# Two of a step's sums of g blocks, moved from VectorE to accumulating DMA transfers

## The chip, the cores and the metric

The kernel runs on one core of a Trainium2 chip. The metric is the device time of one execution in microseconds; the time before is the median of three runs. A profile of one execution shows when each instruction of each engine ran: TensorE (PE, with its weight loads as PEld), VectorE (DVE), ScalarE (ACT), GpSimd (POOL), and SyncE (SP), which only issues transfers.

## The reference

A convolution along the sequence with seven softmax-normalised taps per head, then a feed-forward block without gate or bias; all in float32.

```python
w = softmax(weight, axis=-1)                 # 8 heads x 7 taps
out = einsum('hk,bskhg->bshg', w, x_unf)     # x: 8 x 4096 x 192, causal, 24 columns a head
x2 = out.reshape(32768, 192)
h = x2 @ w_in                                # 192 x 2048
g = h * (1 / (1 + exp(-1.702 * h)))          # quick GELU
return g @ w_out                             # 2048 x 192
```

## The kernel before

The tokens are worked in 32 steps ("big" in the code). A step holds 512 tokens from each half of the batch. Step 0 has a routine of its own (`first_step`, with the loading and rounding of the weights); steps 1 to 31 each run `hidden` twice, with v = 0 and v = 1, and then `second`.

- `hidden(big, v, ...)` makes half of the hidden columns. The products with w_in (line 577, through `product1`) follow a scheme that needs fewer products than blocks and, in exchange, sums of blocks before and after. ScalarE copies (line 607) and VectorE sums (line 611, through `sum2`) put the results together in `room`, and ScalarE's quick GELU writes them to `g` (lines 598 and 600).
- `second(big, ...)` multiplies g with w_out by a scheme on blocks: g is seen as rows 1 to 3 of five 128-row pieces and columns 1 to 4 of 256 tokens, and `block(r, j)` is such a block, 128 partitions x 5 x 256 numbers, 640 KB. Sixteen sums or differences of blocks go before the products p2 to p20. Each product is one call of `go(bank, h, w, t, ...)` (matmuls on line 867): five rounds, or six with `left`, and in each round three matmuls for the product and one of a list of side products, in four column strips of the array.

Every engine's order of work is the order in which the code calls it (`tc.manual_schedule()`); the waits between engines and transfers follow from which tiles are read and written. `work(us)` and `vec_work(us)` put pieces of the next step's convolution between VectorE's sums, as many as fit a stated time.

Around the change, the order is this. Late in `hidden` with v = 1, line 679 makes t_a = block(2,3) - block(3,3), and line 690 sums k18; then line 692 adds block(2,2) into block(2,3), and line 693 makes t_8. Then `give(False, big)` lets line 516 (`cross`) issue copies of the next step's convolved blocks from one half of the partitions to the other, on SyncE's queue; these wait for the last products that read `conv_t`. In `second`, TensorE runs p3, p11, p2 (on t_a), p19 (on block(2,3)), p8, p10, and the product called q13p (on t_a). VectorE meanwhile does lines 893, 896, 897 and 900; line 903, which adds block(2,2) into t_a after p2 has read it; line 908, which reads p8; and line 910, t_8 = t_a - block(3,2). Block (2,2) is rewritten on line 913. GpSimd in these steps adds the convolution's taps (line 505) and sums convolved blocks (lines 388 and 390).

Transfers that add into their destination exist in the kernel before in one place: `add_forms` (line 439), twelve of 240 KB each, issued by GpSimd in step 0.

Of the kernel before, what the change touches and what calls it, by code (L numbers as in the profile page):

```python
# [11 lines left out]
ALU = mybir.AluOpType  # L12
# [3 lines left out]
def kernel(  # L16
# [29 lines left out]
    nc = tc.nc  # L46
# [34 lines left out]
    vec, act = nc.vector, nc.scalar  # L81
# [42 lines left out]
    def block(r, j):  # L124

        n, o = COL[j]
        i = ND * ROW[r]
        return g[:, n, i : i + ND, o * T : (o + 1) * T]

    def rest(j):  # L130
# [16 lines left out]
    t_a, t_8 = (  # L147
        flat_room[:, i * BLK : (i + 1) * BLK].rearrange("p (k t) -> p k t", k=ND) for i in range(2)
    )
# [76 lines left out]
    def form(i):  # L226
        return w_form[:, i, :, :]
# [82 lines left out]
    for c in range(NC):  # L310
        part = sel[:, c, :].rearrange("i (h q) -> i h q", h=2)
        for sign in (1, -1):
            nc.gpsimd.affine_select(
                out=part,
                in_=part,
# [220 lines left out]
    def give(early, big):  # L536
        given[early] = big
        for what in waiting[early]:
            cross(*what)
        waiting[early].clear()  # L540
# [45 lines left out]
    def terms(big, v, slot, *ts, first=False):  # L586
        for t in ts:
            product1(slot, *TERMS[t], big, v, first)
            first = False
# [3 lines left out]
    def gelu(b, u, v, src):  # L593
        m, n = divmod(b, 2)
        i = 2 * (v * len(PAIRS) + PAIRS.index((m, u)))
        if isinstance(src, list):
            for h in range(2):
                act.activation(g[:, n, i + h, :], src[h], AF.Gelu_apprx_sigmoid)  # L598
        else:
            act.activation(g[:, n, i : i + 2, :], src, AF.Gelu_apprx_sigmoid)  # L600
# [4 lines left out]
    def copy2(dst, src):  # L605
        for h in range(2):
            act.copy(bank(dst, h), bank(src, h))  # L607

    def sum2(op, dst, a, b):
        for h in range(2):  # L610
            op(*(bank(t, h) for t in (dst, a, b)))  # L611
# [6 lines left out]
    def hidden(big, v, x, z, y, sums, work, fetch, last=lambda: None):  # L618

        def pe(slot, *ts, first=False):
            terms(big, v, slot, *ts, first=first)


        if v:
            pe(z, 7, first=True)
            give(True, big)
        pe(sums, 12)
        copy2(k15, sums)  # L630
        pe(x, 5, 17)
        gelu(B11, 0, v, x)
        if not v:
            pe(z, 7, first=True)
        pe(sums, 0)
        copy2(k16, sums)
        last()
        def turn_next():
            if big + 2 < N_BIG:
                need(f"done {big + 1}")  # L640
                turn_x(big + 2)

        if v or big == 1:
            work(3.2 if v else 1.6)

        pe(y, 6, 14, first=True)
        sum2(vec.tensor_sub, x, z, k15)
        if v:
            vec.tensor_add(t_s, block(2, 1), block(2, 4))
            vec.tensor_sub(block(2, 1), block(2, 1), block(3, 1))  # L650
        work(2.6 if v else 1.2)
        pe(sums, 13)
        copy2(k19, sums)
        pe(x, 2)
        copy2(k18, x)
        pe(z, 11)
        pe(sums, 20, 10)
        sum2(vec.tensor_sub, k15, y, k19)
        gelu(B12, 0, v, sums)
        pe(x, 4)  # L660
        copy2(k20, x)
        sum2(vec.tensor_sub, k19, z, k19)
        work(1.1)
        gelu(B22, 1, v, k19)
        gelu(B22, 0, v, k15)
        pe(y, 8)
        pe(sums, 1, 9, first=True)
        pe(y, 15)
        if v and big == 1:
            turn_next()  # L670
        else:
            work(2.2 if big > 1 and not v else 1.1)
        sum2(vec.tensor_add, k20, k20, sums)
        sum2(vec.tensor_sub, k16, y, k16)
        gelu(B11, 1, v, k20)
        pe(x, 18)
        gelu(B21, 1, v, x)
        if v:
            vec.tensor_sub(t_a, block(2, 3), block(3, 3))
        fetch()  # L680
        if not v:

            copy2(y, z)
        gelu(B21, 0, v, k16)
        work(1.2)
        if not v and big > 1:
            turn_next()
        pe(sums, 3, 19)
        work(0.7)
        sum2(vec.tensor_add, k18, k18, sums)  # L690
        if v:
            vec.tensor_add(block(2, 3), block(2, 2), block(2, 3))
            vec.tensor_sub(t_8, t_s, block(3, 1))
        return lambda: gelu(B12, 1, v, k18)

# [138 lines left out]
    def second(big, bx, by, bs, vec_work, final, last):  # L834
# [34 lines left out]
        def go(bank, h, w, t, first=True, left=None):  # L869

            dst = bank[0:n3, h * T : (h + 1) * T]
            steps = [(w[:, k, :], t[:, k, :]) for k in range(ND)]
            if left:
                steps.append((w_out_s[:, left[0] - 1, NF - 1, :], rest(left[1])[:, 0, :]))
            for k, (wk, tk) in enumerate(steps):
                for c in range(NC):
                    one_matmul(chunk(dst, c), wk[:, chunk_cols(c)], tk, first and k == 0, k == len(steps) - 1)
                d, ws, ts, st, to = side.pop(0)
                one_matmul(d, ws, ts, st, to is not False)
                if to is not False:  # L880
                    act.copy(to, d)  # L881
                rounds_done[0] += 1
                if rounds_done[0] >= LATE and rounds_done[0] % EVERY == LATE % EVERY:
                    next_tap()
            return dst

        add, sub = vec.tensor_add, vec.tensor_sub
# [12 lines left out]
        sub(block(1, 2), block(1, 2), block(3, 2))  # L900
        p2 = go(m3, 0, w_part(1, 2), t_a)
        act.copy(s2, p2)
        add(t_a, block(2, 2), t_a)
        p19 = go(m2, 1, form(F19), block(2, 3), first=False, left=(2, 3))
        act.copy(s23, p19)
        vec_work(2.8)
# [75 lines left out]
    def work(us):  # L982
        while todo and todo[0][1] <= us + 0.2:
            us -= todo[0][1]
            todo.pop(0)[2]()
# [7 lines left out]
    def need(label):  # L993
        for q in (todo, ready):
            while any(item[0] == label for item in q):
                q.pop(0)[2]()
# [34 lines left out]
    def first_step(fetch):  # L1031
# [35 lines left out]
        plain(0, 0, 1, 0, slots[1], (1, 2), 1)  # L1067
        plain(0, 0, 0, 0, slots[0], (0,), 1)
        conv(0, 0, 0, second, act.mul)
        sign_piece(0, RIGHT[0])  # L1070
        conv(0, 0, 1, second)
        round_w_in(0, *RIGHT)
        conv(0, 0, 2, second)
        split_e(1)
        split_rest(1)
# [80 lines left out]
    def turn_x(big):  # L1156
        for c in range(NC):
            transpose_x(big, c)
        if big + 1 < N_BIG:
            load_x(big + 1)  # L1160
# [5 lines left out]
    def fetch(big, v, slot):  # L1166

        need(f"first {big}")
        terms(big, v, slot, 16, first=True)
# [6 lines left out]
    for big in range(1, N_BIG):  # L1176
        more = big + 1 < N_BIG
        last = hidden(big, 0, x, z, y, sums, work, lambda: fetch(big, 1, z))
        x, z, y, sums = z, x, sums, y
        hidden(big, 1, x, z, y, sums, work, lambda: fetch(big + 1, 0, z) if more else None, last)()  # L1180
        give(False, big)
        if more:
            need(f"all {big + 1}")
        need("forms")
        if big + 2 < N_BIG:
            begin(big + 2)
        second(big, x, y, sums, work, lambda: copy2(sums, z) if more else None, not more)
        x, z = z, x
# [30 lines left out]
```

## Time and profile before

| what | value |
|---|---|
| median of 3 runs | 2314.72 us (2314.16 to 2314.89) |
| span of the profiled execution, first to last instruction | 2312.2 us |
| TensorE busy, share of the span | 2304.8 us, 100% |
| VectorE busy | 2005.1 us, 87% |
| ScalarE busy | 1376.9 us, 60% |
| GpSimd busy | 432.4 us, 19% |
| granted TensorE clock, mean | 1.000 |
| line 692 and line 903 on VectorE | 31 each, 1.48 us each |
| DMA engines, mean | 60 GB/s |

The page gives the profiled execution by its span, 2312.2 us; against the median of the runs, 2.5 us lie around it. Busy time says how long an engine had an instruction in work; matmuls overlap in the array and their ends are modelled, so a busy share of 100% says that TensorE was never without work, not that the array was full. A row of waits gives the engine and line that waited, what ended the wait, the total in us, how often, and the longest. In a row of stretches, the share of DMA is the mean busy share of the core's 16 DMA engines. The landing of a transfer is the time from its issue to the arrival of its last byte.

### The profile page before, as it was taken

How to read it: one execution, taken by the hardware profiler on the slowest of the kernel's cores; microseconds unless marked ns; L12 is line 12 of the kernel's file. 1: busy time of each engine (PE TensorE's matmuls, PEld its weight loads, DVE VectorE, ACT ScalarE, POOL GpSimd, SP SyncE). 2: the span in 40 equal slices, each digit the busy share in tenths (PEclk: the TensorE clock that was granted, in tenths of full speed). 3: DMA queues.
4: the chain of work that ended last, by engine and by line, in shares of the span. 5: the costliest groups of instructions: out<-in, count | busy, mean ns of one | idle time of the engine just before them, and what ended most of it. 6: DMA issues, size and time to landing. Idle time of an engine off the chain costs nothing.

```text
span 2312.2 us, 60320 instructions
## 1 busy us (share of the span) xinstructions
PE 2304.8 (100%) x25982; PEld 1217.8 (53%) x25982; DVE 2005.1 (87%) x2819; ACT 1376.9 (60%) x2554; POOL 432.4 (19%) x451
## 2 busy tenths in 40 slices
PE   9999999999999999999999999999999999999999
PEld 5355555555555555555555555555555555555556
DVE  8898889888898888898888988889888898888877
ACT  7555665566655556555566555665565655556644
POOL 0311222102221022211122211222102221022200
PEclk9999999999999999999999999999999999999999
DMA  8632322223221233112331132321223321231010
GB/s 185 121 67 60 70 52 47 56 57 70 65 48 43 57 70 70 42 43 58 70 70 43 44 69 57 70 53 45 57 57 70 68 45 43 57 70 45 17 43 16
DMA packets 199899, 137.99 MB, mean 60 GB/s; under 512 B 109008, under 2 KB 190544, under 8 KB 195664
## 3 DMA queue, kind: packets, MB, share of 16 engines
q1 hardware_dynamic: 197072, 130.98, 25.7%
q0 software_dynamic: 1728, 2.95, 0.8%
q8 instruction: 204, 3.34, 0.6%
q14 instruction: 63, 0.52, 0.1%
q10 hardware_dynamic: 832, 0.20, 0.0%
HBM read 53.15 MB, written 25.17 MB: 34 GB/s over the span
## 4 chain that ended last, share of the span: by engine, by line
PE 99%; ACT 0%; DVE 0%; DMA 0%; issue 0%; SPq 0%; DVEq 0%; ACTq 0%
PE slot L577 35%; PE slot L867 33%; PE sums L577 16%; PE sums L867 14%; PE slot L746 2%; DMA xin<-in_x_dram 0%; ACT conv_t L1029 0%; DVE xt L471 0%; DVE conv_t L494 0%; SPq L99 0%; ACT conv_t L354 0%; ACT conv_t L353 0%; DVE osbs L819 0%; ACT conv_t L523 0%; ACT conv_t L1025 0%
## 5 line engine op out<-in xcount | busy, mean ns | idle before, releaser
L577 PE MATMUL slot<-conv_t,w_in_s 64*128 64x512 f32 x3740 | 852.5, 590 | 0.3 <-DVE w_in_s L373 0.3
L867 PE MATMUL slot<-g,w_form 128*32 128x256 f32 x6700 | 772.5, 379 | 0.0
L577 PEld LDWEIGHTS slot<-conv_t,w_in_s 64*128 64x128 f32 x3740 | 369.0, 187 | 432.1 <-issue 386.9
L505 POOL TENSOR_TENSOR conv_t<-conv_t,g 128x512 f32<-128x512 f32 x180 | 244.8, 1360 | 1448.6 <-ACT conv_t L501 1436.8
L867 PEld LDWEIGHTS slot<-g,w_form 128*32 128x32 f32 x6700 | 399.6, 110 | 134.9 <-ACT g L598 23.5
L867 PE MATMUL sums<-g,w_form 128*32 128x256 f32 x3530 | 461.8, 379 | 0.0
L867 PE MATMUL slot<-g,w_out_s 128*32 128x256 f32 x4432 | 442.0, 379 | 0.0
L577 PE MATMUL sums<-conv_t,w_in_s 64*128 64x512 f32 x1660 | 405.4, 591 | 0.3 <-DVE w_in_s L373 0.3
L600 ACT ACTIVATE g<-room 128x1024 f32<-128x1024 f32 x310 | 324.5, 1073 | 90.9 <-DVE room L611 90.9
L494 DVE SCALAR_TENSOR_TENSOR conv_t<-xt,cw,conv_t 128x512 f32<-128x512 f32 (+1 forms) x390 | 309.3, 793 | 10.1 <-ACT conv_t L492 3.2
L867 PEld LDWEIGHTS slot<-g,w_out_s 128*32 128x32 f32 x4432 | 226.0, 110 | 97.5
L867 PEld LDWEIGHTS sums<-g,w_form 128*32 128x32 f32 x3530 | 233.3, 110 | 65.6
L607 ACT COPY room<-slot 128x512 f32<-128x512 f32 x434 | 231.5, 602 | 57.3 <-PE slot L577 57.3
L577 PEld LDWEIGHTS sums<-conv_t,w_in_s 64*128 64x128 f32 x1660 | 165.7, 187 | 189.1 <-issue 154.1
L598 ACT ACTIVATE g<-slot 128x512 f32<-128x512 f32 x334 | 179.7, 590 | 88.8 <-PE slot L577 88.8
L881 ACT COPY room<-slot 32x256 f32<-32x256 f32 x245 | 89.8, 367 | 205.8 <-PE slot L867 200.2
L867 PE MATMUL sums<-g,w_out_s 128*32 128x256 f32 x1706 | 205.3, 379 | 0.0
L867 PE MATMUL slot<-room,w_form 128*32 128x256 f32 x2340 | 182.1, 379 | 0.0
L611 DVE TENSOR_TENSOR room<-slot,room 128x512 f32<-128x512 f32 x248 | 156.1, 680 | 20.4 <-ACT room L607 20.4
L611 DVE TENSOR_TENSOR room<-room,sums 128x512 f32<-128x512 f32 x124 | 79.1, 679 | 70.2 <-PE sums L577 70.2
L611 DVE TENSOR_TENSOR room<-room,slot 128x512 f32<-128x512 f32 x124 | 79.1, 678 | 64.5 <-PE slot L577 64.5
L607 ACT COPY room<-sums 128x512 f32<-128x512 f32 x186 | 100.0, 591 | 58.8 <-PE sums L577 58.8
(212 smaller groups left out, 2665.5 us busy)
## 6 DMA issues: line engine op xcount, KB each, us to landing
xin<-in_x_dram SPq DMA_DIRECT2D x240, 180.0 KB, 4.1
conv_t<-conv_t SPq DMA_DIRECT2D x62, 512.0 KB, 6.2
out_dram<-osbs SPq DMA_DIRECT2D x186, 128.0 KB, 2.6
conv_t<-conv_t SPq DMA_DIRECT2D x62, 256.0 KB, 3.1
conv_t<-conv_t SPq DMA_DIRECT2D x62, 64.0 KB, 4.5
xin<-in_x_dram SPq DMA_DIRECT2D x16, 160.0 KB, 3.3
w_form<-w_out_s POOLq DMA_DIRECT2D x7, 240.0 KB, 4.1
osbs<-in_moe_w_out_dram SPq DMA_DIRECT2D x2, 768.0 KB, 8.3
```

The costliest lines, as they stand in the source:

```text
L494: vec.scalar_tensor_tensor(out=dst, in0=src, scalar=tap, in1=dst, op0=ALU.mult, op1=ALU.add)
L505: nc.gpsimd.tensor_add(dst, dst, tap_home(big, k))
L577: nc.tensor.matmul(slot[h], w_in_s[halves[h], a, v * P : (v + 1) * P], src, start=first, stop=True, skip_group_check=True,)
L598: act.activation(g[:, n, i + h, :], src[h], AF.Gelu_apprx_sigmoid)
L600: act.activation(g[:, n, i : i + 2, :], src, AF.Gelu_apprx_sigmoid)
L607: act.copy(bank(dst, h), bank(src, h))
L611: op(*(bank(t, h) for t in (dst, a, b)))
L746: nc.tensor.matmul(chunk(bank, c), w[:, chunk_cols(c)], t, start=first and i == 0, stop=not more and i == len(steps) - 1, skip_group_check ...
L867: nc.tensor.matmul(dst, w, t, start=first, stop=last, skip_group_check=True)
L881: act.copy(to, d)
```

## The change

Line 692 and line 903 become transfers with an accumulating destination, issued by GpSimd. The source is block(2,2) in both; the destination is block(2,3) in the first and t_a in the second. Each moves 128 x 5 pieces of 256 numbers. No other line changes. In the changed program VectorE has 62 instructions fewer and GpSimd 62 transfers more; in GpSimd's order a step's two come behind the sums of lines 388 and 390 and ahead of the next six of line 505. The first matmul of p19 and the first of q13p, which waited for VectorE, now wait for a transfer each; so do line 910 (for the second transfer) and line 913 (for the first), and, in the step that follows, the ScalarE instructions that write the same places of `room` and `g`.

```diff
@@ hidden
         work(0.7)
         sum2(vec.tensor_add, k18, k18, sums)
         if v:
-            vec.tensor_add(block(2, 3), block(2, 2), block(2, 3))
+            nc.gpsimd.dma_start(out=block(2, 3), in_=block(2, 2), accum_op=ALU.add)
             vec.tensor_sub(t_8, t_s, block(3, 1))
         return lambda: gelu(B12, 1, v, k18)
@@ second
         p2 = go(m3, 0, w_part(1, 2), t_a)
         act.copy(s2, p2)
-        add(t_a, block(2, 2), t_a)
+        nc.gpsimd.dma_start(out=t_a, in_=block(2, 2), accum_op=ALU.add)
         p19 = go(m2, 1, form(F19), block(2, 3), first=False, left=(2, 3))
```

## The prediction

> **What bounds the kernel now.** I read the page first, then TensorE's waits, then one middle step in time order (980 to 1035 us), then the DMA engines by stretches. From the page:
>
> ```profile
> span 2312.2 us, 60320 instructions
> PE 2304.8 (100%) x25982; PEld 1217.8 (53%) x25982; DVE 2005.1 (87%) x2819; ACT 1376.9 (60%) x2554; POOL 432.4 (19%) x451
> ```
>
> TensorE is idle 7.4 us in all, at the two ends. The waits of TensorE:
>
> ```profile
> PE sums L453 <- POOL osbs masks.py:199: 1.4, 1, 1.4
> PE slot L577 <- DVE w_in_s L373: 0.3, 1, 0.3
> PE sums L577 <- DVE w_in_s L373: 0.3, 1, 0.3
> PE slot L1011 <- DVE xt L471: 0.2, 1, 0.2
> ```
>
> These are columns of total us, times and longest. That is all: 2.2 us, none of it in the 31 repeated steps. VectorE at 87% holds TensorE up nowhere, so relief for VectorE has nothing to shorten. What counts is when the two sums are ready against when TensorE asks. The step in time order, VectorE's instructions first, then two of TensorE's (start, duration, what):
>
> ```profile
> 986.40 1.48 DVE L679 TENSOR_TENSOR room<-g 128x1280 f32<-128x1280 f32 x1
> 989.43 1.48 DVE L692 TENSOR_TENSOR g<-g 128x1280 f32<-128x1280 f32 x1
> 997.96 1.49 DVE L903 TENSOR_TENSOR room<-g,room 128x1280 f32<-128x1280 f32 x1
> 1002.46 1.48 DVE L910 TENSOR_TENSOR room<-room,g 128x1280 f32<-128x1280 f32 x1
> ...
> 988.12 0.42 PE L867 MATMUL slot<-g,w_form 128*32 128x256 f32 x3
> 993.33 0.39 PE L867 MATMUL slot<-room,w_out_s 128*32 128x256 f32 x3
> ```
>
> `second`'s products start at 988.12. p3 and p11 are six rounds each, and p2 (the row that reads room with w_out_s) starts at 993.33: 12 rounds in 5.2 us, 0.431 us a round. So p2 (5 rounds) ends and p19, which reads block(2,3), starts at 988.12 + 17 x 0.431 = 995.45. Then p19 (6), p8 (5) and p10 (6) put q13p, which reads t_a, at 1002.8.
>
> The DMA engines in stretches of the same step, and in two where GpSimd's accumulating transfers of the weight forms (L439) run (busy of PE, PEld, DVE, ACT, POOL, then clock, DMA share, GB/s):
>
> ```profile
> 987.90:989.40 1.50, 1.50 (x26) 0.81 (x28) 1.18 (x2) 0.40 (x1) 0.00 (x0) 1.00 0.58 191
> 989.40:994.40 5.00, 5.00 (x98) 2.99 (x92) 4.96 (x5) 2.53 (x5) 0.00 (x0) 1.00 0.91 210
> 995.50:1002.80 7.30, 7.30 (x140) 4.41 (x136) 7.19 (x9) 2.70 (x8) 0.00 (x0) 1.00 0.01 2
> 65.60:71.20 5.60, 5.60 (x58) 1.69 (x52) 5.53 (x7) 3.73 (x8) 2.63 (x4) 1.00 1.02 177
> 83.00:91.00 8.00, 8.00 (x72) 2.28 (x68) 7.16 (x18) 3.02 (x6) 0.69 (x1) 1.00 1.07 212
> 2308.00:2310.00 2.00, 0.00 (x0) 0.00 (x0) 0.49 (x2) 0.00 (x0) 0.00 (x0) 1.00 0.67 136
> 2310.00:2312.20 2.20, 0.00 (x0) 0.00 (x0) 0.00 (x0) 0.00 (x0) 0.00 (x0) 0.50 0.28 55
> ```
>
> ```profile
> L516 SPq DMA_DIRECT2D conv_t<-conv_t x4: 462/529/596, 985.7 to 988.8; - x4
> DMA to landing us min/median/max: 3.0/4.9/6.3
> ```
>
> ```profile
> L439 POOL DMA_DIRECT2D w_form<-w_out_s x7: 859/1210/1902, 64.1 to 79.0; - x7
> DMA to landing us min/median/max: 3.2/4.8/10.0
> ```
>
> The first pair is the half-to-half copies of line 516 at this step's place (985 to 990 us), the second the forms' transfers of line 439, seven of the twelve in its row. The reader is to see that the engines are 91% busy with line 516 just where the first new transfer must run, and empty where the second must.
>
> **The change part by part.** *Removed:* 31 x 2 sums of VectorE, 62 x 1.48 = 92 us of its 2005. Worth nothing on the path, since no wait of TensorE ends on VectorE in a step. It could give at most TensorE's idle 7.4 us, of which the tail and the start are not touched.
>
> *GpSimd issues two transfers a step.* Its nearest work ends at 973.2 (the sums of line 390 and a memset) and resumes at 1022.4 (L505, after 49 us idle). So both find it idle, and what queues behind them on GpSimd, L505, is not due for 20 us. Descriptor writing: a row of L439 is 0.86 us for 128 rows of 1,920 bytes; the new ones have 640 pieces of 1 KB. If that grew fivefold it would be 4.3 us, 3.4 more; it runs beside data already moving, so I book nothing and look at it again below.
>
> *Length of one new transfer.* 640 KB = 655,360 bytes. Four L439 transfers queued together moved in the stretch 65.60 to 71.20 at 177 GB/s with the engines full: by bytes 655,360 / 177 = 3.7 us. By pieces: 4 x 128 pieces over 16 engines is 32 each in 5.60 us, 0.175 us a piece; 40 pieces each make 7.0 us. I take 4.3, near the bytes, because the x loads in this step come in 640-byte pieces and still move 232 to 270 GB/s, so a short piece adds little; 40 x 0.015 us is my estimate for it. Around it: issue at 64.1 to data at 65.6 is 1.5 us; the shortest landing, 3.2, less 1.5 and a quarter of 5.60 leaves 0.3 after the last byte.
>
> *First transfer, L692.* It waits for L679, which reads block(2,3): 986.40 + 1.48 = 987.9, data from 989.4. Alone it lands at 989.4 + 4.3 + 0.3 = 994.0, before p19's 995.45. But line 516 wants 5.0 x 0.91 = 4.55 us of the same engines. Added up, 989.4 + 4.55 + 4.3 + 0.3 = 998.55, 3.1 us late. By bytes: 1.05 MB of line 516 plus 0.655 at 212 GB/s (83 to 91 us, where both kinds ran together) is 8.0 us, plus 0.6 for short pieces: 998.3, 2.9 late. Taken 3.0. Low end: all at 270 GB/s, the x loads' best, gives 6.3 us and 996.0, 0.55 late. High end: 7.0 us of transfer, 1001.25, 5.8 late. TensorE runs in order: behind p19's first matmul everything stands, p8 to p18 and the next step, and VectorE and ScalarE wait for those.
>
> [...]
>
> *Second transfer, L903.* It overwrites t_a, so it waits for p2's last read, about 995.6, which the first one's lateness doesn't move. Its data follow the first's: from 998.2, plus 4.3 + 0.3 = 1002.8, where q13p is now due at 1002.8 + 3.0 = 1005.8. Hidden, as long as the first is late; with the engines at 0.01 nothing else delays it. With 3.4 us of slow descriptor writing it would land at 1005.1, still hidden. L910 on VectorE waits for it too, but only after L908, which needs p8 (at 1000.2, now 1003.2). Cover gone (first transfer in time): 995.6 + 1.5 + 4.3 + 0.3 = 1001.7, still in time; at 7.0 us, 1.6 late.
>
> *Line 516's own delay:* the copies land some 3 us later, by about 998; the next step's products begin at 1023. Nothing.
>
> *Sum.* 30 steps x 3.0 (the last step has no line-516 copies, and its first transfer lands in time) = 90 us. The profiled execution's span is 2312.2, the median of the runs 2314.7, so 2.5 us lie around the span; 2312.2 + 90 + 2.5 = **2405 us**. A measurement of this kernel can tell about 0.2%, 4.6 us.
>
> **The rivals.** *The clock falls in the stalls.* The last matmul ends at 2306.9, and the clock's row reads 1.00 until 2310.0 and 0.50 after: 3.1 us of idleness were enough. A stall of 3.0 is at that edge. TensorE's first matmul is at 1.4 us and the trace's first record of a full clock at 6.0, so each fall could cost half of 4.6 us, 2.3: 31 x 2.3 = 71 more, 2476. Against: 3.0 falls short of 3.1. [...]
>
> *Pieces, not bytes, set the transfer's time.* 7.0 us and 5.8 late in 30 steps: 174, 2489. For: each 1,920-byte piece holds an engine 0.175 us and the trace has no other size of accumulate. The second then lands at 1000.95 + 7.3 = 1008.3, against 1008.6: hidden still.
>
> *Not slower: the first transfer lands in time.* If the engines served GpSimd's queue first, it would land at 994.0 and line 516 would be late instead, for nobody; the second lands at 1001.7. Then 2314.7. It decides at a landing 7.5 us after issue. Against: L439's transfers landed up to 10.0 us after issue beside line 516, at less than half the bytes. Faster would need a wait on VectorE that the trace doesn't show.
>
> **How the numbers follow.** Forecast (stall 0.55 to 4.5, clock held) 0.62, its own range 2335 to 2450; clock 0.14; pieces 0.16; in time 0.08, of which faster 0.02. The range 2335 to 2490 leaves out the in-time case, about half of the pieces' case and the worst of the clock's, some 0.18. Faster by over 0.2%: 0.02; within: 0.06; slower: 0.92.
>
> **What would show it.** TensorE's waits should have a new row, L867 waiting for the DMA into g, some 30 times 3.0 us, and none or little for the DMA into room. L692's landing should be near 10.7 us, L903's near 7; VectorE's busy time 92 us less; the clock's row 9 throughout. Wrong if L692 lands within 7.5 us of issue, if the waits fall on q13p, if the clock's row drops, or if the delays sit elsewhere.

## The result and the profile after

The changed kernel takes **2514.8 us** (median of 4 runs, 2502.87 to 2520.75) against 2314.78 for the kernel before (2314.16 to 2314.89): 1.0859 times as long, interval 1.0832 to 1.0886. The forecast was 2405, with a range up to 2490. The profiled execution took 2512.5 us. All ratios here and below are of fast executions; two of the kernel before, at 4985 and 6350 us on one chip, are left out as slow. The page of the changed kernel, span and busy times:

```profile
span 2510.7 us, 60417 instructions
PE 2375.6 (95%) x25982; PEld 1273.2 (51%) x25982; DVE 1936.6 (77%) x2757; ACT 1376.8 (55%) x2554; POOL 526.2 (21%) x513
```

TensorE, which was never without work, is now idle for 135 us and, with the same 25982 matmuls, is busy 71 us longer. Those are two losses. The first is in TensorE's waits (total us, times, longest):

```profile
PE sums L867 <- DMA g<-g: 61.4, 15, 4.4
PE slot L867 <- DMA g<-g: 57.2, 15, 4.5
PE slot L867 <- issue: 8.1, 1, 8.1
```

The transfer into g is line 692's; p19 waits for it in every step. The row "issue" is the first step, whose transfer lands 15.3 us after its issue. Together 126.7 us. No row names the transfer into room, line 903's. The instructions and landings of the two lines:

```profile
L692 POOL DMA_DIRECT2D g<-g x31: 1499/1499/1520, 132.2 to 2470.4; - x31
DMA to landing us min/median/max: 6.9/11.2/15.3
...
L903 POOL DMA_DIRECT2D room<-g x31: 1499/1499/1648, 140.0 to 2477.2; - x31
DMA to landing us min/median/max: 6.5/7.0/11.1
```

The second loss shows in one step by stretches (busy of PE, PEld, DVE, ACT, POOL, then clock, DMA share, GB/s). Line 679 ends at 1065.65, p19 is due at 1073.3, and its transfer lands at 1076.83:

```profile
1066.70:1071.70 5.00, 5.00 (x100) 2.99 (x92) 4.96 (x5) 2.53 (x5) 1.00 (x1) 1.00 0.98 205
...
1073.40:1077.00 3.60, 0.07 (x8) 0.07 (x6) 3.49 (x5) 0.37 (x1) 1.50 (x1) 0.88 1.04 159
1077.00:1080.90 3.90, 3.90 (x40) 2.07 (x44) 0.61 (x1) 0.37 (x1) 0.00 (x0) 0.50 0.96 140
1080.90:1083.00 2.10, 2.10 (x28) 1.08 (x24) 0.00 (x0) 0.37 (x1) 0.00 (x0) 0.51 0.00 0
1083.00:1090.00 7.00, 7.00 (x136) 4.34 (x132) 3.97 (x5) 2.54 (x7) 0.00 (x0) 1.00 0.01 2
```

The granted clock falls to half inside the stall, at 1076.1, and stays there until 1083.0: 40 matmuls in 3.90 us, then 136 in 7.00 at the full clock. The 6 us of work from 1077 to 1083 lose 3. Over the whole trace the clock is low in 28 such stretches, each 3.4 or 6.8 us long, and once after the last matmul. The low time outside TensorE's idle time is 133 us, at half speed a loss of some 67. So of 198.5 us (2510.7 - 2312.2), 126.7 are waits, about 67 the clock, and about 5 are not accounted for by either.

Why the transfer is late is in the DMA rows of two stretches of the same step, 1065.7 to 1070.5 and 1072.7 to 1077.5 (queue, packets, MB, share of the 16 engines; q1 carries line 516's copies, q0 GpSimd's transfers):

```profile
q1 hardware_dynamic: 202, 1.00, 86.3%
...
q0 software_dynamic: 780, 0.78, 106.6%
```

SyncE issues line 516's four copies at 1063.46, 1063.96, 1066.07 and 1066.57, the two larger ones last; GpSimd issues its transfer at 1066.20. In the first stretch not one packet of GpSimd's moves; in the second it moves nearly alone. The packet records of the 29 middle steps show the change: a transfer's records close with 16 of 4 bytes, and GpSimd's first piece starts within 0.02 us of the first closing record of the last copy, in every one of these steps. In them the two don't share the engines: one waits for the other. The fourth copy goes ahead although its issue began 0.37 us behind GpSimd's, so the instant of issue is not the place in the order; with the engines free, GpSimd's data begin only 2.1 us after its issue (the copies moved, below).

### The profile page after: what moved, and what is told of

Its sections match the earlier page's. It is cut to its first block, busy times and chain, and to the rows that moved or that the text cites. A ratio compares the mean times of both kernels' runs of the same rounds, so it can differ in the third digit from the quotient of the medians.

```text
span 2510.7 us, 60417 instructions
## 1 busy us (share of the span) xinstructions
PE 2375.6 (95%) x25982; PEld 1273.2 (51%) x25982; DVE 1936.6 (77%) x2757; ACT 1376.8 (55%) x2554; POOL 526.2 (21%) x513
## 3 DMA queue, kind: packets, MB, share of 16 engines
q0 software_dynamic: 42400, 43.59, 11.5%
## 4 chain that ended last, share of the span: by engine, by line
PE 85%; DMA 13%; issue 1%; ACT 0%; DVE 0%; SPq 0%; DVEq 0%; ACTq 0%
PE slot L577 32%; PE slot L867 26%; PE sums L577 14%; DMA g<-g 13%; PE sums L867 11%; PE slot L746 2%; DMA xin<-in_x_dram 0%; ACT conv_t L1029 0%; DVE xt L471 0%; DVE conv_t L494 0%; SPq L99 0%; ACT conv_t L354 0%; ACT conv_t L353 0%; DVE osbs L819 0%; ACT conv_t L523 0%
## 5 line engine op out<-in xcount | busy, mean ns | idle before, releaser
L867 PE MATMUL slot<-g,w_form 128*32 128x256 f32 x6700 | 838.0, 403 | 65.3 <-DMA g<-g 57.2
L867 PE MATMUL sums<-g,w_form 128*32 128x256 f32 x3530 | 506.3, 411 | 61.4 <-DMA g<-g 61.4
L867 PEld LDWEIGHTS slot<-g,w_form 128*32 128x32 f32 x6700 | 426.8, 116 | 211.9 <-issue 92.1
L867 PE MATMUL slot<-g,w_out_s 128*32 128x256 f32 x4432 | 448.1, 383 | 0.0
L867 PEld LDWEIGHTS sums<-g,w_form 128*32 128x32 f32 x3530 | 255.6, 118 | 136.7 <-issue 88.0
L494 DVE SCALAR_TENSOR_TENSOR conv_t<-xt,cw,conv_t 128x512 f32<-128x512 f32 (+1 forms) x390 | 310.1, 795 | 10.2 <-ACT conv_t L492 3.2
L867 PEld LDWEIGHTS slot<-g,w_out_s 128*32 128x32 f32 x4432 | 241.0, 111 | 93.8 <-issue 4.5
L908 DVE TENSOR_TENSOR room<-slot,room 96x256 f32<-96x256 f32 x31 | 13.1, 421 | 229.2 <-PE slot L867 229.2
L867 PE MATMUL slot<-room,w_form 128*32 128x256 f32 x2340 | 187.3, 385 | 0.0
L692 POOL DMA_DIRECT2D g<-g x31 | 46.6, 1503 | 521.9 <-PE sums L577 233.4
L867 PEld LDWEIGHTS slot<-room,w_form 128*32 128x32 f32 x2340 | 109.7, 114 | 66.2 <-issue 10.9
## 6 DMA issues: line engine op xcount, KB each, us to landing
g<-g POOLq DMA_DIRECT2D x31, 640.0 KB, 11.2
```

Source lines behind the costliest of these rows:

```text
L494: vec.scalar_tensor_tensor(out=dst, in0=src, scalar=tap, in1=dst, op0=ALU.mult, op1=ALU.add)
L692: nc.gpsimd.dma_start(out=block(2, 3), in_=block(2, 2), accum_op=ALU.add)
L867: nc.tensor.matmul(dst, w, t, start=first, stop=last, skip_group_check=True)
L908: sub(v8, p8, s12)
```

## The experiments

Times are medians, each against the kernel before on the same chip, whose medians were 2314.1 to 2314.4; ratios carry their intervals. "+x" is us after line 679's end in a step; in the changed kernel p19 is due at about +7.65.

### Each transfer alone, and neither

In the first, line 903 is a VectorE sum again; in the second, line 692 is; in the third both lines are left out.

```diff
 k1_first_only
-        nc.gpsimd.dma_start(out=t_a, in_=block(2, 2), accum_op=ALU.add)
+        add(t_a, block(2, 2), t_a)
 k2_second_only
-            nc.gpsimd.dma_start(out=block(2, 3), in_=block(2, 2), accum_op=ALU.add)
+            vec.tensor_add(block(2, 3), block(2, 2), block(2, 3))
 k3_none
-            nc.gpsimd.dma_start(out=block(2, 3), in_=block(2, 2), accum_op=ALU.add)
-        nc.gpsimd.dma_start(out=t_a, in_=block(2, 2), accum_op=ALU.add)
```

> Only line 692 is a transfer; line 903 stays on VectorE. Theory: the first transfer, which lands behind the half-to-half copies, makes the whole loss (126 us of waits and about 67 us of half clock after them): 2500 to 2520 us, waits of p19 on the transfer 3.6 to 4.5 us a step. Rival, the second transfer has a share of its own: between 2330 and 2480.

> Only line 903 is a transfer; line 692 stays on VectorE. Theory: the engines are free, so it lands 6.5 to 7 us after its issue, that is 14.9 to 15.4 us after line 679's end, and q13p is due at 14.9: waits of 0 to 0.5 us a step, clock full, 2315 to 2331. Rival, the second transfer has a share of the loss that the first one's lateness hid: over 2350.

> Both sums are left out altogether, so block(2,3) and t_a lack block(2,2); no transfer takes their place. Theory: VectorE's 92 us are worth nothing, 2314 to 2316, within 0.2% of before. Rival, VectorE holds TensorE up somewhere that the waits do not show: below 2310.

Measured: the first alone 2507.54, ratio 1.0825 (1.0794 to 1.0856); the second alone 2320.3, 1.0027 (1.0016 to 1.0038); neither 2314.59, 1.0001 (0.9992 to 1.0011). TensorE's waits with the first alone:

```profile
PE sums L867 <- DMA g<-g: 59.7, 15, 4.8
PE slot L867 <- DMA g<-g: 56.7, 15, 5.0
PE slot L867 <- issue: 7.7, 1, 7.7
```

and with the second alone:

```profile
PE slot L867 <- DMA room<-g: 2.5, 4, 1.0
PE sums L867 <- DMA room<-g: 0.3, 2, 0.2
```

Nearly the whole loss is the first transfer's. The second, with the first not late, lands between +14.4 and +16.1 against q13p's due time of +14.9; steps in which it is in time take 71.35 us, as before the change. Without either sum VectorE is busy 1927.3 us instead of 2005.1, and the kernel gains nothing: VectorE's relief has no worth here.

### The clock apart from the wait: dummy matmuls in the stall

Eight rounds of matmuls, whose results nothing reads, are put ahead of p19.

```diff
 k4_warm
+        for _ in range(8):
+            for c in range(NC):
+                one_matmul(chunk(m1[0:n3, 0:T], c), form(F11)[:, 0, chunk_cols(c)], block(3, 2)[:, 0, :], True, True)
         p19 = go(m2, 1, form(F19), block(2, 3), first=False, left=(2, 3))
```

> The changed kernel, with eight rounds of matmuls (3.45 us at full clock) ahead of p19 that nobody reads: they overwrite the place that p8 starts anew. Theory, the idle time of TensorE lets the clock fall, which makes a third of the loss: the wait shrinks to 0.2 to 1 us, the clock stays full, the landing stays at 11 to 12 us after line 679, and the time is 2435 to 2455 although TensorE does 107 us more work. Rival, the loss is the lateness alone and the clock's fall costs little: 2500 or more.

Measured: 2454.46, ratio 1.0608 (1.0592 to 1.0624). TensorE's waits, and the clock of the profiled execution:

```profile
PE slot L867 <- DMA g<-g: 10.1, 12, 1.7
PE sums L867 <- DMA g<-g: 9.9, 14, 1.4
PE slot L867 <- issue: 5.1, 1, 5.1
```

```profile
core 0: 2453.0 us, clock 0.998
```

With 31 x 8 x 0.431 = 107 us more of TensorE's work the kernel is 60 us *faster* than the changed one. The landings are what they were (median 11.3 us after issue). The wait of 126.7 us is now 107 of dummy work and 25 of waits, some 5 more, so the gain is not in the wait but in the clock: before the last matmul it falls in the first step and in no other. 2514.8 + 5 - 67 makes 2453, and that is the clock's share of the loss.

### Line 516's copies out of the way

`give(False, big)` goes from the main loop into `second`, behind `act.copy(q13, q13p)`, where both transfers are done with; ScalarE issues the copies.

```diff
 k5_copies_late
-    def cross(big, b0, b1):
+    def cross(big, b0, b1, queue=nc.sync):
...
         act.copy(q13, q13p)
+        give(False, big, act)
...
-        give(False, big)
```

> The changed kernel with the four half-to-half copies of line 516 that follow each hidden issued by ScalarE behind its copy of q13p, so that the engines are free for both transfers. Theory, the copies ahead of it on the engines make the first transfer late: it lands 6.9 us after its issue as it does in the last step, where no copies run, 7.5 us after line 679's end against 7.65 due; waits of 0 to 0.7 us a step, clock full, 2315 to 2338 us. Rival, the accumulate or its descriptors are slow by themselves: over 2400.

Measured: 2330.46, ratio 1.0069 (1.0049 to 1.0089), mean clock 1.000. Line 692's landing has a median of 6.8 us after issue instead of 11.2, its data begin 2.1 us after issue instead of 5.5. Steps in which both transfers are in time (+6.95 and +14.79 in one) take 71.35 us, exactly the time before; others wait up to 1.8 us, for the second more than for the first. So lateness behind line 516, and the clock that falls with it, make 184 of the 200 us that the change costs; what remains is 0.7%, of which TensorE's waits for the two transfers are 10.7 us. As the steps in time are as long as before, the transfers' traffic by itself costs TensorE nothing there.

### Sharing, pieces, or order?

Two kernels tell apart why the transfer waits. In the first, the two larger copies of a step are cut into two of half the columns each, so that their pieces are shorter. In the second, the copies keep their size but are issued behind the transfer, by ScalarE, after `act.copy(s21, p3)`.

```diff
 k6_short
+        cols = (slice(0, T // 2), slice(T // 2, T)) if b1 - b0 == 8 else (slice(0, T),)
...
-                out=conv_t[halves[1 - o], 1, b0:b1, :], in_=own(big)[halves[o], b0:b1, :]
+                    out=conv_t[halves[1 - o], 1, b0:b1, c], in_=own(big)[halves[o], b0:b1, c]
 k9_copies_behind
         act.copy(s21, p3)
+        give(False, big, act)
...
-        give(False, big)
```

> The changed kernel with the two copies of eight blocks cut into pieces of 512 bytes (four transfers of half the columns in place of two), the same bytes. Theory A, an engine does what was handed to it first: the first transfer's data still begin 5.5 us after its issue, it lands 11 to 12 us after line 679, 2500 to 2525 us. Theory B, the queues take turns piece by piece, so that 8 KB pieces crowd out 1 KB pieces: data begin 2 to 3 us after issue, landing at 9 to 10.5, waits of 1.5 to 3, clock mostly full, 2360 to 2420.

> The changed kernel with the same four copies issued by ScalarE behind its copy of p3, some 3 us after the first transfer's issue in place of beside it. Theory A, an engine does what was handed to it first: the transfer, whose data begin 2.1 us after issue, is little delayed, lands 7.5 to 8.3 us after line 679, waits of 0 to 0.7, 2315 to 2338; the second transfer may now be the late one, behind the copies, with waits of 1 to 3 on q13p, up to 2410. Theory B, turns piece by piece with the 4 and 8 KB pieces of the copies: the first lands at 9 to 12, and the waits stay on p19, over 2360.

Short pieces: 2444.18, ratio 1.0571 (1.0511 to 1.0631), between the expectations. Line 692 (694 in this kernel's file) still lands late:

```profile
L694 POOL DMA_DIRECT2D g<-g x31: 1499/1499/1517, 132.2 to 2419.6; - x31
DMA to landing us min/median/max: 6.9/10.3/11.6
```

In a step of it, SyncE issues the four half-size copies at +0.41, +1.07, +1.75 and +3.94, GpSimd the transfer at +0.55. The data of the first two come first and end between +4 and +6.5, as the engines finish one after the other; the transfer's data begin at +3.9 to +4.3 in most steps; the last two copies' data come behind it, at +7.5 to +11.5. What moved the transfer forward by some 2 us is not that pieces alternate: fewer copies had been handed over before it. Here too the copy at +1.07, 0.52 us behind the transfer's issue, went first, and the one at +1.75 did not.

Copies issued behind the transfer: 2433.58, ratio 1.052 (1.0502 to 1.0538). Line 692 is undisturbed at the median, although the copies are issued at +3.2 and later, while its data run (+2.6 to +6.8):

```profile
L692 POOL DMA_DIRECT2D g<-g x31: 1499/1499/1520, 132.2 to 2390.8; - x31
DMA to landing us min/median/max: 6.6/6.7/8.9
```

In the stretch where its data run, 1037.7 to 1041.5 in one step, all the data packets are GpSimd's:

```profile
q0 software_dynamic: 625, 0.64, 116.7%
q10 hardware_dynamic: 1, 0.00, 0.5%
```

Now the second transfer is behind the copies and lands at +17.9 to +19.2 in all steps but the last, 10 us after issue at the median, and ScalarE, held by issuing four copies (4.86 us in one step), is late with the copy sc12:

```profile
PE slot L867 <- DMA room<-g: 27.7, 14, 2.6
...
PE slot L867 <- ACT spare L900: 15.8, 12, 2.9
```

So in these runs the order in which transfers are handed over decides, in both directions (line 692's landing 11.2 us after issue behind the copies and 6.7 ahead of them, line 903's 7.0 and 10), and the loss only changed its place. The second transfer's waits were expected, at 1 to 3 us a step; the time is above the 2410 that was expected at most because ScalarE's lateness (31.2 us of waits for line 900 in two rows) and eight falls of the clock came on top.

### Moving due times instead

Five kernels put other products ahead of the ones that wait, with the copies as in the changed kernel (the first) or moved (the others).

```diff
 k7_reorder             p8, p10 ahead of p19
 k8_both                the same, copies by ScalarE behind q13, p15 starting its sum anew
 k11_all_covered        p8 ahead of p19, p20 ahead of q13p, copies by ScalarE behind q13
 k12_all_covered        p8, p19, p20, p10, q13p; copies by ScalarE behind q13
 k13_copies_gpsimd      as k12_all_covered, copies by GpSimd at that place of the code
```

> The changed kernel with p8 and p10, which need neither transfer, ahead of p19, 4.74 us of matmuls. Theory, the loss is a due time missed by 3.6 to 4.5 us: p19 is now due 12.4 us after line 679, the transfer lands at 11.2 to 12.2, so no wait there; q13p is due at 14.9 as before and the second transfer lands at 14.9 to 15.8, waits of 0 to 0.9; clock full, 2318 to 2340. Rival, the transfers disturb TensorE or VectorE in another way: over 2400.

> The changed kernel with both remedies: the four copies issued by ScalarE behind its copy of q13p, and p8 and p10 ahead of p19 (p15 then starts its place anew, so that every result is that of the reference). The first transfer lands at about 7.5 us and is due at 12.4, the second at 14.0 to 15.5 and is due at 14.9. Theory, all that the change cost is the lateness and the clock behind it, and all that it can give is nothing: waits of 0 to 0.5 us on q13p, 2314 to 2325 us. Rival, 40 MB more through the DMA engines or two more instructions on GpSimd cost something besides: over 2330.

> The changed kernel with the four copies issued by ScalarE behind its copy of q13p, p8 ahead of p19 and p20 ahead of q13p. The first transfer lands 7 to 8.7 us after line 679 and is due at 9.8, the second at 14.4 to 16.4 and is due at 17.1: both covered in every step. Theory, the change costs its lateness and the clock behind it and nothing besides, and the time taken off VectorE gives nothing: no waits on transfers, full clock, 2314 to 2318 us. Rival, the transfers' traffic or GpSimd's instructions cost something besides: 2323 or more. Second rival, VectorE's free time gives something once nothing waits: under 2311.

> As the run before, but with the order p8, p19, p20, p10, q13p, so that two products in a row never share a bank of PSUM and TensorE need not wait for a reader of it; VectorE adds p20 into s23 before line 910. The first transfer is due 9.7 us after line 679 and the second 17.1, against landings of 7 to 8.7 and 14.4 to 16.4. Theory, the change costs its lateness and the clock behind it and nothing besides, and the time taken off VectorE gives nothing: no waits on transfers, full clock, 2314 to 2319 us. Rival, the transfers' traffic costs something besides: 2323 or more. Second rival, VectorE's free time gives something: under 2311.

> The order p8, p19, p20, p10, q13p as in the run before, with the four copies issued by GpSimd right behind its second transfer in place of ScalarE, whose issuing held up its side copies of line 881 (a gap of 1.26 us a step on TensorE). If an engine does first what was handed to it first, the second transfer is not delayed by copies that come behind it. Theory, the change costs its lateness and the clock behind it and nothing besides: no waits on transfers nor on ScalarE, full clock, 2314 to 2319 us. Rival, the transfers' traffic costs something besides, or the copies delay the second transfer: 2323 or more. Second rival, VectorE's free time gives something: under 2311.

In the first two of these the products that share p19's PSUM bank don't add up to the reference's sums, since their order in it is changed; that part of the computation differs.

| kernel | us | ratio (interval) | what TensorE still waits for |
|---|---|---|---|
| p8, p10 first | 2338.56 | 1.0104 (1.0087 to 1.0122) | transfers: 10.2 us in all |
| the same, copies late | 2329.43 | 1.0065 (1.0051 to 1.0078) | the second transfer: 5.9 us |
| p8 first, p20 before q13p | 2375.84 | 1.0268 (1.0254 to 1.0282) | no transfer; readers of a shared bank: 28 us |
| p8, p19, p20, p10 | 2347.43 | 1.0144 (1.0127 to 1.016) | no transfer; line 881: 15 us |
| the same, GpSimd issues | 2339.11 | 1.0105 (1.0088 to 1.0122) | no transfer by name; line 933 of its file, on VectorE: 5.9 us; nothing that the profile shows: 6.2 us |

The first hit its expectation: line 692 lands as late as in the changed kernel (median 11.4 us after issue), but p19 is now due at +12.4, and with the stall the clock's loss goes too. The other four missed: the second lies 4 us above its range, and the last three fell where the rival was expected by which the traffic costs something besides. Two ran into orders of my own making: p10 directly behind p19 has to wait until the copies have read the bank they share (the 28 us of the table), and copies issued by ScalarE hold up its small copies of line 881, 0.5 us a step on average (14.9 us in 30 waits) and 1.3 at most:

```profile
PE slot L867 <- ACT room L881: 8.1, 15, 1.3
```

The waits are not the whole loss of the last three. TensorE is also busy 2335.0, 2322.9 and 2316.9 us in their traces, against 2304.8 before, for the same matmuls at a full clock; why was not tried. Against the rival speak the steps of 71.35 us with both transfers in time, above. No version beat the kernel before; the changed kernel's best is the second transfer alone, 2320.3. What a version would take in which everything is covered and nothing else is moved was not reached.

## Why the prediction was wrong

- **Where and in which direction: right.** TensorE waits at p19 for the transfer into g, in each step with copies of line 516, and in the last step, without copies, for 0.7 us only. VectorE's relief is worth nothing (neither sum: 2314.59). The second transfer costs nothing behind the late first one: taking it away gains 7 us of 2514.8, with overlapping spreads of runs (2493.96 to 2510.99 against 2502.87 to 2520.75). It lands 7.0 us after issue, as said. The copies' own delay hurts nobody.
- **The transfer's length: right.** 4.3 us were booked. 40 packets per engine at a median 0.109 us make 4.4 (at their shortest, 0.101 us, 4.0), and with the copies moved the median from the first piece to the last closing record is 4.2. The 0.015 us a piece in the 4.3 was an estimate that no row showed; with the 3.7 us by bytes, 0.093 a piece, it makes 0.108. So the rival of 0.175 us a piece was wrong; the 1,920-byte pieces took 0.168 and are 1.9 times as long. The way to the first piece was mis-sized, without effect behind the copies: 1.5 us after line 679 were booked, and undisturbed it is 2.6 (issue at +0.55, data 2.07 later).
- **The stall's size: the step "added up" failed.** It gave 3.0 us; measured are 3.5 to 4.5 in the 29 middle steps, 118.6 us in all with the 0.7 of the last, and 8.1 in the first. It treated the 16 engines as one pool: copies for 4.55 us from +1.5, then the transfer for 4.3, landed at +10.65. That the copies go first was in effect assumed rightly; that all engines change over together was not. In the packet records of those steps the copies' last pieces end at +6.0 on the earliest engine and at +7.65 on the latest (medians), where the sum had +6.05 for all. The transfer, spread over all 16, lands with the latest: 7.65 + 4.4 = +12.05, against +11.2 to +12.2 measured. The last of its 16 closing records comes at a median of +11.4, the first already at +9.3, so the engines that change over first stand free for the second transfer.
- **The clock: the step "3.0 falls short of 3.1" failed twice.** 3.1 us was the idle time at one fall, at the kernel's end, and served as a threshold. Over five traces (the changed kernel, the first transfer alone, dummy matmuls, short pieces, copies behind) there was no fall in or right behind the 61 stalls of 0.5 to 1.8 us, but 4 in 16 from 1.8 to 2.2, 12 in 16 from 2.2 to 3.0, 5 in 9 from 3.0 to 3.5, and 63 in 71 longer ones; in the kernel with the copies behind, a stall of 2.0 us was enough in three of the 15 of 1.8 to 2.2 us. So even the booked 3.0 us would have lost the clock in many steps, and at 4.1 us it fell in nearly all. The price was right: 2.3 us a fall were estimated, 67 / 28 = 2.4 were lost. That is luck in part: the estimate stood on one start of 4.6 us, and the low stretches are 3.4 or 6.8 long. The rival's chance, 0.14, was too low, and its time of 2476 stood on the stall of 3.0. Put together, 29 x 4.1 + 8.1 + 28 x 2.4 = 194, and 2314.7 + 194 = 2509: the high end of 2490 lacked the case in which the longer stall and the clock come together.
- **The announced sign for the clock was blunt.** In the row of 40 slices of the page every digit is still 9, with 28 falls in it; a mean of 0.967 rounds away there. The stretches and the mean clock of the core show it.
- **VectorE's busy time** fell by 68.5 us, not 92: 31 x 2 x 1.48 went, and its other instructions took 23 us longer. Why was not tried, and nothing waits for it.

## What to carry to other kernels

A transfer that must be on time has to be handed over before the bulk transfers of its surroundings, or well after them. In these runs copies issued 0.4 and 0.5 us behind it still went ahead, and copies issued 2.6 us behind did not. Count its data, on the engine that is free last, from the end of everything handed over before it (here 7.65 + 4.4 = +12.05, against +11.2 to +12.2 measured); this held between GpSimd's queue and those of SyncE and ScalarE. A stall of TensorE had two prices here, its length and the clock: in the five traces the clock fell in none of the 61 stalls of 0.5 to 1.8 us, in 4 of 16 from 1.8 to 2.2 and in 63 of the 71 above 3.5, and a fall cost some 2.4 us in the changed kernel. Add the two up, and never keep them as alternatives. VectorE, busy 87% with no wait of TensorE ending on it in a step, gave nothing when it was relieved (2314.59 against 2314.22): look first for what waits for an engine.

## What was not expected of the hardware

- In these runs a DMA engine did not share between GpSimd's packets and those of SyncE or ScalarE that it had been handed earlier. First data came 5.5 us after issue behind line 516's copies and 2.1 us without, and copies issued 2.6 us behind the transfer left it alone (landing 6.7). Turns of one piece are not seen in these runs, but turns of many pieces are not decided against: the copies that the transfer waited for put 8 pieces on an engine in the changed kernel and 64 in the one with short pieces, the transfer itself 40. Where the order is kept, the runs do not show.
- Issuing a transfer of 640 pieces took GpSimd 1.50 us, the shortest of line 439's, of 128 pieces, 0.86; what GpSimd does in that time ("descriptor writing" in the prediction) no trace shows. ScalarE, issuing four copies of line 516, was blocked for 4.86 us in one step of the kernel with the copies behind.
- The middle steps of the changed kernel take 75.1 to 78.7 us. The shorter low stretches last 3.413 us, and the starts of the 28 falls lie whole multiples of it apart, each from the one before within 0.001 us. A step of 78.5 is 23 such stretches, and many falls of the clock follow each other at that distance (1076.1, 1154.6, 1233.1, 1311.7): this grid of the clock and the loss it causes may hold the steps in a rhythm. That the one sets the other was not tried.
